# Global attention tasks without TensorE transposes: 32x32 blocks on VectorE, a pass through DRAM, and all later transfers in written order

## The chip, the core and the metric

The program runs on one core of a Trainium2 chip. A core has a matrix engine (TensorE, PE in the profile, with its weight loads as PEld), VectorE (DVE), ScalarE (ACT), GpSimd (POOL) and a queue engine (SyncE, SP) that here issues nearly every DMA. The metric is the device time of one execution in microseconds, the median of several. The kernel before took 911.14 us (three runs, 910.88 to 911.96); the one execution that was profiled took 908.84 us, of which 907.1 us lie between its first and last instruction (its span).

## The reference

Sliding-window attention with a few global tokens, then a feed-forward network with a parametric ReLU, all in float32. There are 8 batches and 8 heads, 512 local and 32 global tokens, head dimension 64. Each global query sees all 544 keys, each local query the 32 global keys and the local keys within 32 positions.

```python
s_g = scale * np.matmul(q_g, k_all.transpose(0, 1, 3, 2))
out_g = np.matmul(sm(s_g), v_all)                 # global queries: 544 keys
...
mask = np.abs(pos[:, None] - pos[None, :]) <= window
s_ll = np.where(mask, s_ll, -1000000000.0)
a_l = sm(np.concatenate([s_lg, s_ll], axis=-1))   # local queries: 32 global + band
out_l = np.matmul(a_l, np.concatenate([v_g, v_l], axis=2))
...
h = x @ w_in                                      # 4352 x 512 by 512 x 2048
g = np.maximum(h, 0.0) + alpha * np.minimum(h, 0.0)
return g @ w_out
```

## The kernel before

**The feed-forward part** sets the beat. Tokens come in nine groups: group b (0 to 7) is the 512 local tokens of batch b, group 8 the 256 global tokens of all batches. A group is worked off in 16 chunks of 128 hidden units; T = 16 * group + chunk numbers the steps. In step T TensorE makes the chunk's hidden values (`f1`: 12 matmuls into a PSUM bank `h_ps`, three for each quarter of the model dimension, because each float32 product is split into a rounded part and a rest: tiles `xh`, `xl`, `wt`), ScalarE and VectorE apply the parametric ReLU (`leak`, `bend`: tile `g`), ScalarE rounds it (`gh`), GpSimd makes the rest (`gl`), and TensorE adds the chunk of two steps ago to the output banks `o` (`f2`: 8 matmuls with `gh`, then 4 with `gl`). When a group is done its four `o` banks are copied to tiles `ost` and stored.

**Local attention** runs between these matmuls, by pairs P of heads, four pairs to a batch, 32 in all. Pairs 0 to 7 go by TensorE transposes; from pair 8 on (`NRAW`) VectorE turns the probabilities in 32x32 blocks (`give`: tile `pb`), SP writes that to DRAM and reads it back with the blocks in their places (`take`: tile `pt`, four transfers for each head), and the values' weighted sum (`local_values`, PSUM tile `o_ps`) follows some steps later. The outputs go the same way (`xb`, then `x_raw`). Inputs of a pair are `qk` (672 KB, one buffer from pair 4 on) and `vw` (two transfers of 512 KB, one buffer from pair 4 on).

**Global attention** is 16 tasks k of two head pairs each. `global_scores` fills part of two PSUM tiles `g_ps` with a large negative number (VectorE memset), multiplies queries and keys (`gn`), and makes row maxima, exponentials (into `sg_sb`, which lies in the buffer of `gn`) and reciprocals of the sums. `global_transposes` turns the probabilities with four 128x128 TensorE transposes into a PSUM tile `gt`, which ScalarE and VectorE copy to `sgt_sb`; the last 32 keys are turned by VectorE directly. `global_values` multiplies with `vg` into `go`, and ScalarE scales it into the two diagonal blocks of `og_sb`, whose other blocks are zero. `global_outputs` turns that on TensorE by a matmul with a matrix `pick` of two unit matrices (`gx`), and ScalarE copies it to `x_glb`, the input of group 8.

**What sets the order.** Up to step 18 a string `ORDER` writes it out: a letter and a number for each piece (S scores, R maxima, E exponentials, V values, F `f1`, A and B the two halves of `f2`, r `leak`, g `bend`, d and e the two heads of `local_exchange`, G `global_scores`). After that TensorE's order is the program's; the piece of a pair or task is put into a step ahead of `f2`'s first half ("pre" before `f1`, "mid") or between its halves ("post"). VectorE, ScalarE and GpSimd are then ordered by a scheduler that simulates the program at build time, with a higher priority for attention. For SP the same holds: after its first loads `dma.on` is False, so that the scheduler places the transfers, except inside `local_exchange`, which switches it on and back. Each queue runs its instructions strictly in order, so that a transfer that waits holds up all behind it. Tiles of 128x512 share one pool of 21 buffers; `h_ps`, `o_ps` and `go` share two PSUM banks, `s_ps`, `g_ps`, `gt` and `gx` two others.

Pair P's values stand in step T = 4 * (P - 4), "post", and behind them the scores of pair P + 1. Task k's scores stand in "mid" of step u, its values in "mid" of step v, the next task's u. Before the change:

```python
plan(u - 2, "mid", load_gn, k)
plan(u, "mid", global_scores, k)
plan(u + 1, "mid", load_vg, k)
plan(v - 2, "mid", global_transposes, k)
at.setdefault((v, "mid"), []).insert(0, (global_values, k))
plan(v + 1, "mid", global_outputs, k)
```

Nearly all instructions are issued through small helpers, so the profile's lines are theirs: L78 is VectorE, ScalarE and SP, L109 TensorE's matmuls, L112 its transposes, L475 GpSimd's `gl`. Tiles tell them apart.

Of the kernel before, what the change touches and what calls it, by code (L numbers as in the profile page):

```python
# [8 lines left out]
F32 = mybir.dt.float32  # L9
# [5 lines left out]
ALU = mybir.AluOpType  # L15
# [18 lines left out]
PAD = (32, 32)  # L34
# [12 lines left out]
    N7 k15 l14 X7 B11 s15 x7 H13 F14 H12 j15 A12 L12 u15 r14 l15 B12 g14 F15 d8 e8 L13 A13 r15 H14  # L47
    g15 H15 B13 L15 L14 F16 r16 g16 H16 L16 A14 V8 S9 B14 N8 R9 F17 p9 r17 q9 g17 d9 A15 B15 e9 H17
# [36 lines left out]
def longformer_ffn(ctx: ExitStack, tc: tile.TileContext, qk, vs, gn, vg, w, alpha, out):  # L85
# [22 lines left out]
    def matmul(*a, **k):  # L108
        return tc.keep_in_program_order(nc.tensor.matmul(*a, **k))  # L109

    def transpose(*a):
        return tc.keep_in_program_order(nc.tensor.transpose(*a))  # L112
# [13 lines left out]
    def bank(tag, name):  # L126
        return psum.tile([128, 512], F32, tag=tag, name=name, bufs=2 if tag in "hs" else 1)
# [20 lines left out]
    vec.tensor_tensor(pick, ident[:, 0:64], ident[:, 64:128], op=ALU.add)  # L148
# [3 lines left out]
    nc.gpsimd.memset(og_sb, 0.0)  # L152
# [148 lines left out]
    def local_exchange(P, heads=(0, 1)):  # L301
        on, dma.on = dma.on, True
        for h in heads:
            ps_of[P, h] = give(pr_of.pop((P, h)), "pb")
        if 1 in heads:
            for h in range(2):
                pt_of[P, h] = stage("pt")
                take(pt_of[P, h], ps_of.pop((P, h)))
        dma.on = on
# [49 lines left out]
    gns, vgs, sgs, gz = {}, {}, {}, {}  # L359
# [13 lines left out]

    def global_scores(k):
        ss = [bank("s", "g_ps") for h in range(2)]
        for h in range(2):
            vec.memset(ss[h][64:128, 256:288], -3.0e38)
# [21 lines left out]
        vec.tensor_copy(z[64:128, 2:4], z[0:64, 2:4])  # L399
        gz[k] = z  # L400

    def global_transposes(k):
        ps, sg_sb = bank("s", "gt"), sgs.pop(k)
        for h in range(2):
            for e in range(2):
                c = 256 * h + 128 * e
                transpose(ps[:, c : c + 128], sg_sb[:, h, 128 * e : 128 * e + 128], ident)
        for h in range(2):
            dst = sgt_sb[:, 0:4, h].rearrange("k (r e) n -> k r e n", r=2)
            copy("ad"[h], dst, ps[:, 256 * h : 256 * h + 256].rearrange("k (e r n) -> k r e n", e=2, r=2))  # L410
# [192 lines left out]
    others = {"R": local_maxima, "E": local_exps, "C": local_copies, "N": local_weights, "x": round_x, "y": rest_x, "D": local_exchange, "p": lambda P: local_exps(P, (0,)), "q": lambda P: local_exps(P, (1,)), "d": lambda P: local_exchange(P, (0,)), "e": lambda P: local_exchange(P, (1,)), "G": global_scores, "h": take_high, "k": take_low, "s": shift, "j": first_join, "u": upper, "l": lower, "r": leak, "g": bend, "H": round_g, "L": rest_g}  # L603
# [81 lines left out]
```

## Time and profile before

| | |
|---|---|
| median of three runs | 911.14 us |
| the profiled execution | 908.84 us |
| its span, first to last instruction | 907.1 us |
| TensorE busy | 889.9 us (98%) |
| VectorE busy | 439.0 us (48%) |
| ScalarE busy | 387.7 us (43%) |
| GpSimd busy | 163.3 us (18%) |
| granted TensorE clock, mean | 0.994 |
| DMA, bytes moved | 140.33 MB |

A row of the groups' view names line, engine, operation, out<-in, partitions x elements, then the count, busy time in us, mean ns of one, and the engine's idle time before them with what ended it. A row of the timeline has start and duration in us, engine, line, operation, tiles, and in brackets the idle time before it and what ended it. Matmuls overlap, so a matmul's cost is the distance from its start to the next one's. One float32 matmul that isn't rounded stands as two instructions. The table by stretches gives, for each, its length, then each engine's busy time with its instructions in brackets, the granted clock, the DMA engines' busy share and GB/s.

### The profile page before, as it was taken

The page shows a single profiled execution, that of the slowest core. Times are in us where ns is not written, and L with a number is a line of the kernel's source. Part 1 is how long each engine was busy: PE and PEld are TensorE (multiplying, and loading weights), DVE is VectorE, ACT ScalarE, POOL GpSimd, SP SyncE. Part 2 cuts the span into 40 slices and gives each one's busy share as a digit, 9 for nine tenths or more (in the row PEclk, how much of TensorE's full clock was granted, in tenths as well). Part 3 has the DMA queues.
Part 4 walks back from the last instruction along what each step waited for, and adds up shares of the span by engine and source line. Part 5 has one row for each costly group of instructions (what it writes and reads, how often), then busy time and mean ns, then how long its engine had stood idle before and what let it go on. Part 6 is the DMA issues. An engine that isn't in the chain of part 4 may idle for free.

```text
span 907.1 us, 21212 instructions
## 1 busy us (share of the span) xinstructions
PE 889.9 (98%) x8704; PEld 718.6 (79%) x8704; DVE 439.0 (48%) x840; ACT 387.7 (43%) x1078; POOL 163.3 (18%) x158
## 2 busy tenths in 40 slices
PE   8889999999999999999999999999999999999998
PEld 4568787787878778877888788877887888888898
DVE  6899996455454444454354434554454323111311
ACT  5786783334443334443343344343343233222322
POOL 3000000211212122112111221122112222222221
PEclk9999999999999999999999999999999999999999
DMA  9994235565446543754546454664535320100000
GB/s 329 342 408 189 81 110 166 183 203 182 159 143 209 183 155 123 246 192 160 180 147 211 149 171 148 213 205 164 185 123 180 112 93 24 46 1 1 12 36 25
DMA packets 139953, 140.33 MB, mean 155 GB/s; under 512 B 9296, under 2 KB 112208, under 8 KB 137808
## 3 DMA queue, kind: packets, MB, share of 16 engines
q1 hardware_dynamic: 139568, 138.72, 45.6%
q8 instruction: 68, 1.11, 0.5%
q14 instruction: 29, 0.24, 0.1%
q10 hardware_dynamic: 288, 0.26, 0.1%
HBM read 111.16 MB, written 27.79 MB: 153 GB/s over the span
## 4 chain that ended last, share of the span: by engine, by line
PE 92%; DMA 3%; SPq 3%; DVE 2%; ACT 0%; issue 0%; DVEq 0%
PE o L109 41%; PE h_ps L109 40%; PE s_ps L109 4%; PE o_ps L109 3%; SPq L78 3%; DMA qk<-in_qk_dram 2%; PE go L109 1%; PE g_ps L109 1%; DMA ws<-in_w_dram 1%; DVE wt L78 1%; PE gt L112 1%; PE pt L112 0%; PE gx L109 0%; ACT wt L78 0%; DVE xl L78 0%
## 5 line engine op out<-in xcount | busy, mean ns | idle before, releaser
L109 PE MATMUL h_ps<-xh,wt 128*128 128x512 f32 (+1 forms) x1152 | 340.0, 378 | 0.0
L475 POOL TENSOR_TENSOR gl<-g,gh 128x512 fp32r<-128x512 f32 (+1 forms) x128 | 156.0, 1219 | 737.0 <-ACT gh L78 632.5
L109 PE MATMUL o<-gh,wt 128*128 128x512 f32 (+1 forms) x1152 | 277.7, 383 | 0.0
L78 DVE SCALAR_TENSOR_TENSOR g<-g,beta_sb,h_ps 128x512 f32<-128x512 f32 (+1 forms) x144 | 102.3, 711 | 317.5 <-ACT g L78 316.2
L109 PEld LDWEIGHTS h_ps<-xh,wt 128*128 128x128 f32 x1152 | 212.0, 188 | 41.9 <-DVE wt L78 0.4
L109 PEld LDWEIGHTS o<-gh,wt 128*128 128x128 f32 x1152 | 204.7, 188 | 44.2 <-issue 6.3
L109 PE MATMUL h_ps<-xl,wt 128*128 128x512 f32 (+1 forms) x576 | 217.7, 378 | 0.0
L78 ACT ACTIVATE g<-h_ps 128x512 f32<-128x512 f32 (+1 forms) x144 | 82.1, 571 | 263.0 <-PE h_ps L109 228.4
L109 PE MATMUL o<-gl,wt 128*128 128x512 f32 (+1 forms) x576 | 151.3, 384 | 0.2 <-DVE gl L78 0.2
L109 PEld LDWEIGHTS h_ps<-xl,wt 128*128 128x128 f32 x576 | 108.4, 188 | 20.0
L78 ACT CAST gh<-g 128x512 fp32r<-128x512 f32 (+1 forms) x144 | 85.7, 597 | 87.3 <-DVE g L78 81.9
L109 PEld LDWEIGHTS o<-gl,wt 128*128 128x128 f32 x576 | 102.9, 188 | 23.4 <-issue 4.4
L78 ACT ACTIVATE p<-p,mn 128x128 f32<-128x128 f32 x192 | 74.5, 390 | 103.3 <-DVE mn L78 70.8
L78 DVE STREAM_TRANSPOSE pb<-p 128x512 f32<-128x512 f32 x48 | 34.1, 711 | 44.0 <-ACT p L78 43.2
L109 PEld LDWEIGHTS o_ps<-vw,pt 128*32 128x32 f32 x2048 | 31.3, 112 | 13.9 <-issue 7.2
L78 DVE TENSOR_TENSOR xq<-o_ps,rz 128x512 f32<-128x512 f32 x32 | 22.1, 691 | 40.0 <-PE o_ps L109 39.2
L109 PE MATMUL s_ps<-qk 64*32 64x128 f32 x2048 | 37.8, 278 | 0.6 <-DMA qk<-in_qk_dram 0.6
L109 PE MATMUL o_ps<-vw,pt 128*32 128x64 f32 x2048 | 36.7, 224 | 1.6 <-DMA pt<-pb 1.6
L78 ACT ACTIVATION_READ_ACCUMULATOR p<-p,mn 128x1 f32 x192 | 36.0, 188 | 0.0
L109 PEld LDWEIGHTS s_ps<-qk 64*32 64x32 f32 x2048 | 29.1, 107 | 6.6 <-issue 2.5
L78 DVE TENSOR_REDUCE mn<-p 128x4 f32<-128x512 f32 x48 | 30.5, 660 | 0.1
L78 DVE SCALAR_TENSOR_TENSOR p<-s_ps,mask 128x512 f32<-128x512 f32 x48 | 30.2, 664 | 0.0
(83 smaller groups left out, 541.2 us busy)
## 6 DMA issues: line engine op xcount, KB each, us to landing
vw<-in_vs_dram SPq DMA_DIRECT2D x64, 512.0 KB, 5.3
qk<-in_qk_dram SPq DMA_DIRECT2D x32, 672.0 KB, 6.6
ws<-in_w_dram SPq DMA_DIRECT2D x16, 1024.0 KB, 9.6
pb<-pb SPq DMA_DIRECT2D x48, 256.0 KB, 2.3
pt<-pb SPq DMA_DIRECT2D x192, 64.0 KB, 2.0
vg<-in_vg_dram SPq DMA_DIRECT2D x32, 320.0 KB, 3.5
gn<-in_gn_dram SPq DMA_DIRECT2D x32, 288.0 KB, 4.4
out_dram<-ost SPq DMA_DIRECT2D x32, 256.0 KB, 3.4
```

What stands on the lines that cost most here:

```text
L78: ins = call(*a, **k)
L109: return tc.keep_in_program_order(nc.tensor.matmul(*a, **k))
L112: return tc.keep_in_program_order(nc.tensor.transpose(*a))
L475: (vec if T < NF else nc.gpsimd).tensor_tensor(gl[:, 0:n], gs.pop(T)[:, 0:n], gh_of[T][:, 0:n].bitcast(F32), op=ALU.subtract)
```

## The change

Six things are changed.

1. `global_transposes` has no TensorE part. VectorE turns the two heads' 256 columns in 32x32 blocks into a tile `sgb` of the common pool (two instructions), SP writes it to DRAM (256 KB) and reads it into `sgt_sb` with four transfers of 64 KB. The layout of `sgt_sb` changes with it. It stands in step u + 1 in place of v - 2.
2. `global_outputs` is eight 32x32 VectorE transposes from `og_sb` to `x_glb` in place of a matmul and a copy; `og_sb` is 64 columns, scaled by one ScalarE instruction in place of two; `pick` and the zeroing of `og_sb` are gone.
3. `global_fill`, the memset of `g_ps`, is a piece of its own: in step u - 1, "post", and for the first task (`f0`) ahead of `H17`.
4. `local_exchange` leaves `dma.on` True: from its first use on (`d8`) SP's transfers stand in the order in which the program writes them.
5. The loads of pair 9's `vw` and pair 10's `qk` stand behind `F18`; `gn` of task k + 1 is loaded behind task k's transposes and `vg`.
6. `d8 e8` stand ahead of `g14 F15` in place of behind them.

```diff
-    N7 k15 l14 X7 B11 s15 x7 H13 F14 H12 j15 A12 L12 u15 r14 l15 B12 g14 F15 d8 e8 L13 A13 r15 H14
-    g15 H15 B13 L15 L14 F16 r16 g16 H16 L16 A14 V8 S9 B14 N8 R9 F17 p9 r17 q9 g17 d9 A15 B15 e9 H17
+    N7 k15 l14 X7 B11 s15 x7 H13 F14 H12 j15 A12 L12 u15 r14 l15 B12 d8 e8 g14 F15 L13 A13 r15 H14
+    g15 H15 B13 L15 L14 F16 r16 g16 H16 L16 A14 V8 S9 B14 N8 R9 F17 p9 r17 q9 g17 d9 A15 B15 e9 f0 H17
...
     def local_exchange(P, heads=(0, 1)):
-        on, dma.on = dma.on, True
+        dma.on = True
...
-        dma.on = on
...
+    def global_fill(k):
+        gps[k] = [bank("s", "g_ps") for h in range(2)]
+        for h in range(2):
+            vec.memset(gps[k][h][64:128, 256:288], -3.0e38)
...
     def global_scores(k):
-        ss = [bank("s", "g_ps") for h in range(2)]
-        for h in range(2):
-            vec.memset(ss[h][64:128, 256:288], -3.0e38)
+        ss = gps.pop(k)
...
     def global_transposes(k):
-        ps, sg_sb = bank("s", "gt"), sgs.pop(k)
+        sg_sb, blk = sgs.pop(k), stage("sgb")
+        for h in range(2):
+            dst = blk.rearrange("k (b h c n) -> k h c b n", b=4, h=2, c=2)[:, h]
+            vec.transpose(dst, sg_sb[:, h, 0:256].rearrange("q (c b n) -> q c b n", c=2, b=4))
         for h in range(2):
             for e in range(2):
-                c = 256 * h + 128 * e
-                transpose(ps[:, c : c + 128], sg_sb[:, h, 128 * e : 128 * e + 128], ident)
-        for h in range(2):
-            dst = sgt_sb[:, 0:4, h].rearrange("k (r e) n -> k r e n", r=2)
-            copy("ad"[h], dst, ps[:, 256 * h : 256 * h + 256].rearrange("k (e r n) -> k r e n", e=2, r=2))
-            for e in range(2):
-                vec.transpose(sgt_sb[0:32, 4, h, 32 * e : 32 * e + 32], sg_sb[32 * e : 32 * e + 32, h, 256:288])
+                vec.transpose(sgt_rest[0:32, h, 32 * e : 32 * e + 32], sg_sb[32 * e : 32 * e + 32, h, 256:288])
+        spread = dram.tile([128, 4, 128], F32, tag="sgb", name="sgb", bufs=2)
+        dma.dma_start(spread, blk.rearrange("k (b n) -> k b n", b=4))
+        for b in range(4):
+            dma.dma_start(sgt_main[32 * b : 32 * b + 32].rearrange("k (w n) -> k w n", w=4), spread[:, b].rearrange("(w k) n -> k w n", w=4))
...
         z = gz.pop(k)
-        for h in range(2):
-            hs = slice(64 * h, 64 * h + 64)
-            act.activation(og_sb[hs, hs], ps[hs, 0:64], AF.Copy, scale=z[hs, 2 + h : 3 + h])
+        act.activation(og_sb, ps[:, 0:64], AF.Copy, scale=z[:, 2:3])
 
     def global_outputs(k):
-        ps = bank("s", "gx")
         b, p = divmod(2 * k, NPAIR)
-        matmul(ps[:, 64:128], og_sb, pick, start=True, stop=True)
-        act.copy(x_glb[:, p : p + 2, SG * b : SG * b + SG], ps[:, 64:128].rearrange("d (e q) -> d e q", e=2))
+        for h in range(2):
+            for e in range(2):
+                for i in range(2):
+                    r0, q0 = 64 * h + 32 * i, 64 * h + 32 * e
+                    vec.transpose(x_glb[r0 : r0 + 32, p + e, SG * b : SG * b + SG], og_sb[q0 : q0 + 32, 32 * i : 32 * i + 32])
...
         if k:
-            plan(u - 2, "mid", load_gn, k)
+            plan(u - 1, "post", global_fill, k)
             plan(u, "mid", global_scores, k)
+        plan(u + 1, "mid", global_transposes, k)
         plan(u + 1, "mid", load_vg, k)
-        plan(v - 2, "mid", global_transposes, k)
+        if k + 1 < NPR // 2:
+            plan(u + 1, "mid", load_gn, k + 1)
         at.setdefault((v, "mid"), []).insert(0, (global_values, k))
-        plan(v + 1, "mid", global_outputs, k)
+        at.setdefault((v + 1, "mid"), []).insert(0, (global_outputs, k))
...
     def first_scores(P, warm):
         local_scores(P, warm)
-        if P > NRAW:
-            load_v(P)
-        if P >= NPAIR:
+        if NPAIR <= P <= NRAW:
             load_qk(P + 1)
...
         if T == NF:
             load_gn(0)
+        if T == NF + 2:
+            load_v(NRAW + 1)
+            load_qk(NRAW + 2)
```

How the built programs' orders differ is shown at three places. First SP in the steady part, from the loads of one pair to those of the next task, as it was and as it is now. Names are those of the tiles: `xb` and `x_raw` carry a pair's outputs, `pb` and `pt` the next pair's probabilities, `vw` and `qk` its values and the inputs of the pair after it.

```order
L78 DMA vw<-in_vs_dram 128x8x128 x2
L78 DMA xb<-xb 128x512
L78 DMA qk<-in_qk_dram 128x1344
L78 DMA x_raw<-xb 32x4x128 x4
L78 DMA pb<-pb 128x512 x2
L78 DMA pt<-pb 32x4x128 x8
L78 DMA vg<-in_vg_dram 128x640 x2
L78 DMA gn<-in_gn_dram 128x576 x2
```

```order
L78 DMA xb<-xb 128x512
L78 DMA x_raw<-xb 32x4x128 x4
L78 DMA pb<-pb 128x512 x2
L78 DMA pt<-pb 32x4x128 x8
L78 DMA vw<-in_vs_dram 128x8x128 x2
L78 DMA qk<-in_qk_dram 128x1344
L78 DMA sgb<-sgb 128x512
L78 DMA sgt_sb<-sgb 32x4x128 x4
L78 DMA vg<-in_vg_dram 128x640 x2
L78 DMA gn<-in_gn_dram 128x576 x2
```

The loads `vw` and `qk` have moved from ahead of the outputs and the probabilities to behind them, and five transfers of the task have come in ahead of `vg` and `gn`. Where a group ends, its four stores `out_dram<-ost` now stand between `qk` and `sgb`.

Second VectorE where pair 8's probabilities are turned (`d8 e8`), as a piece of the difference; `wt` is the last chunk's weights, `xl` the rest of group 1's inputs.

```order
 L78 TENSOR_TENSOR gl<-g,gh 128x512
 L78 TENSOR_TENSOR wt<-wt 128x2x512
+L78 STREAM_TRANSPOSE pb<-p 128x4x4x32 x2
 L78 SCALAR_TENSOR_TENSOR g<-g,beta_sb,h_ps 128x512
 L78 TENSOR_TENSOR xl<-x_raw,xh 128x512 x4
-L78 STREAM_TRANSPOSE pb<-p 128x4x4x32 x2
 L78 TENSOR_TENSOR gl<-g,gh 128x512
 L78 SCALAR_TENSOR_TENSOR g<-g,beta_sb,h_ps 128x512
```

The two transposes have moved ahead of one `bend` and four `xl`.

Third TensorE at the first task's transposes, before and now; `o_2171` and the like are output banks of the feed-forward part.

```order
L109 MATMUL h_ps<-xl,wt 128x512
L112 MATMUL gt<-ident,gn 128x128 x4
L109 MATMUL o_2171<-gh,wt 128x512 x2
L109 MATMUL o_2172<-gh,wt 128x512 x2
L109 MATMUL o_2173<-gh,wt 128x512 x2
L109 MATMUL o_2174<-gh,wt 128x512 x2
L109 MATMUL o_ps<-vw,pt 32x64 x32
```

```order
L111 MATMUL h_ps<-xl,wt 128x512
L111 MATMUL o_2168<-gh,wt 128x512 x2
L111 MATMUL o_2169<-gh,wt 128x512 x2
L111 MATMUL o_2170<-gh,wt 128x512 x2
L111 MATMUL o_2171<-gh,wt 128x512 x2
L111 MATMUL o_ps<-vw,pt 32x64 x32
L111 MATMUL s_ps<-qk 32x128 x32
```

The four transposes are gone, and so is the matmul `gx<-pick,og_sb` of each task at another place; nothing else on TensorE has changed its place.

More of the change, by code (lines that the diff above doesn't have):

```diff
@@ L33 @@
 HPU = 4
-PAD = (32, 32)
+PAD = (32, 32, 0)
 LAG = 2
@@ L99, in longformer_ffn @@
     beta_sb = const.tile([128, NF], F32, name="beta_sb")
-    pick = const.tile([128, 64], F32, name="pick")
-    og_sb = const.tile([128, 128], F32, name="og_sb")
-    sgt_sb = const.tile([128, 5, 2, 64], F32, name="sgt_sb")
+    og_sb = const.tile([128, 64 + PAD[2]], F32, name="og_sb")[:, 0:64]
+    sgt_sb = const.tile([128, 640], F32, name="sgt_sb")
+    sgt_main = sgt_sb[:, 0:512]
+    sgt_cut = sgt_main.rearrange("k (r e h c n) -> k r e h c n", r=2, e=2, h=2, c=2)
+    sgt_rest = sgt_sb[:, 512:640].rearrange("k (h n) -> k h n", h=2)
     x_raw = const.tile([128, NPAIR, SL], F32, name="x_raw")
@@ L147, in longformer_ffn @@
     vec.tensor_scalar(beta_sb, alpha_sb, -1.0, 1.0, op0=ALU.mult, op1=ALU.add)
-    vec.tensor_tensor(pick, ident[:, 0:64], ident[:, 64:128], op=ALU.add)
     band(mask_bf.rearrange("q (i n) -> q i n", i=4), -8.0 * NEG)
@@ L151, in longformer_ffn @@
     nc.gpsimd.memset(sgt_sb, 0.0)
-    nc.gpsimd.memset(og_sb, 0.0)
     def keep_warm(ps, n, add=False):
@@ L357, in rest_x @@
         vec.tensor_tensor(xl, ps_of.pop(P), xh.bitcast(F32), op=ALU.subtract)
-    gns, vgs, sgs, gz = {}, {}, {}, {}
+    gns, vgs, sgs, gz, gps = {}, {}, {}, {}, {}
     big = []
@@ L419, in global_values @@
                     q0 = 64 * h + 32 * e
-                    matmul(ps[q0 : q0 + 32, 0:64], sgt_sb[:, y, h, 32 * e : 32 * e + 32], vgs[2 * k + e][:, y, 64 * h : 64 * h + 64], start=(y == 0), stop=(y == 4))
+                    wt = sgt_cut[:, y // 2, e, h, y % 2] if y < 4 else sgt_rest[:, h, 32 * e : 32 * e + 32]
+                    matmul(ps[q0 : q0 + 32, 0:64], wt, vgs[2 * k + e][:, y, 64 * h : 64 * h + 64], start=(y == 0), stop=(y == 4))
         for e in range(2):
@@ L423, in global_values, with global_outputs @@
         z = gz.pop(k)
+        act.activation(og_sb, ps[:, 0:64], AF.Copy, scale=z[:, 2:3])
+    def global_outputs(k):
+        b, p = divmod(2 * k, NPAIR)
         for h in range(2):
-            hs = slice(64 * h, 64 * h + 64)
-            act.activation(og_sb[hs, hs], ps[hs, 0:64], AF.Copy, scale=z[hs, 2 + h : 3 + h])
-    def global_outputs(k):
-        ps = bank("s", "gx")
-        b, p = divmod(2 * k, NPAIR)
-        matmul(ps[:, 64:128], og_sb, pick, start=True, stop=True)
-        act.copy(x_glb[:, p : p + 2, SG * b : SG * b + SG], ps[:, 64:128].rearrange("d (e q) -> d e q", e=2))
+            for e in range(2):
+                for i in range(2):
+                    r0, q0 = 64 * h + 32 * i, 64 * h + 32 * e
+                    vec.transpose(x_glb[r0 : r0 + 32, p + e, SG * b : SG * b + SG], og_sb[q0 : q0 + 32, 32 * i : 32 * i + 32])
     def split_x(G, c):
@@ L602, in longformer_ffn @@
     on_tensor = {"S": first_scores, "T": local_transposes, "V": first_values, "X": local_outputs, "F": first_f1, "A": lambda T, n: f2(T, 0, n), "B": lambda T, n: f2(T, 1, n)}
-    others = {"R": local_maxima, "E": local_exps, "C": local_copies, "N": local_weights, "x": round_x, "y": rest_x, "D": local_exchange, "p": lambda P: local_exps(P, (0,)), "q": lambda P: local_exps(P, (1,)), "d": lambda P: local_exchange(P, (0,)), "e": lambda P: local_exchange(P, (1,)), "G": global_scores, "h": take_high, "k": take_low, "s": shift, "j": first_join, "u": upper, "l": lower, "r": leak, "g": bend, "H": round_g, "L": rest_g}
+    others = {"R": local_maxima, "E": local_exps, "C": local_copies, "N": local_weights, "x": round_x, "y": rest_x, "D": local_exchange, "p": lambda P: local_exps(P, (0,)), "q": lambda P: local_exps(P, (1,)), "d": lambda P: local_exchange(P, (0,)), "e": lambda P: local_exchange(P, (1,)), "f": global_fill, "G": global_scores, "h": take_high, "k": take_low, "s": shift, "j": first_join, "u": upper, "l": lower, "r": leak, "g": bend, "H": round_g, "L": rest_g}
     for word in ORDER.split():
```

2 lines of the change are left out of this document (1 added, 1 removed).

## The prediction

> **What bounds the kernel now.** I read first the busy shares and the chain that ended last, then the table by stretches, then TensorE's timeline around the pieces that the change touches.
>
> ```profile
> PE 889.9 (98%) x8704; PEld 718.6 (79%) x8704; DVE 439.0 (48%) x840; ACT 387.7 (43%) x1078; POOL 163.3 (18%) x158
> PE 92%; DMA 3%; SPq 3%; DVE 2%; ACT 0%; issue 0%; DVEq 0%
> ```
>
> TensorE is busy for 98% of the span and makes 92% of the chain. Where its idle time lies, the stretches tell.
>
> ```profile
> 0.00:150.00 150.00, 139.77 (x1623) 103.94 (x1624) 130.29 (x184) 108.09 (x258) 7.27 (x30) 0.97 0.67 238
> 150.00:168.00 18.00, 14.74 (x195) 11.35 (x194) 9.81 (x19) 7.01 (x24) 1.95 (x2) 1.00 0.59 195
> 168.00:745.00 577.00, 577.00 (x5952) 464.65 (x5952) 265.80 (x586) 229.66 (x712) 116.46 (x91) 1.00 0.52 170
> ```
>
> From 168 to 745 us, where 15 of the 16 global tasks' scores and all their transposes lie, TensorE has no gap (577.00 of 577.00) at a granted clock of 1.00, while VectorE works 265.80 us, under half. A matmul that leaves this stretch shortens it by its own start-to-start distance, so long as nothing new makes TensorE wait. Just ahead of it, from 150 to 168, TensorE idles 3.26 us.
>
> **The change part by part.** *The task's TensorE work.* Two groups leave, 64 transposes `gt` and 32 instructions `gx`:
>
> ```profile
> L112 PE MATMUL gt<-ident,gn 128*128 128x128 f32 x64 | 9.6, 271 | 0.0
> L109 PE MATMUL gx<-pick,og_sb 128*128 128x64 f32 x32 | 5.3, 247 | 0.0
> 206.78:232.69 25.91, 25.91 (x284) 20.70 (x283) 12.12 (x29) 9.57 (x32) 5.14 (x4) 1.00 0.54 177
> 257.27:283.66 26.39, 26.39 (x288) 21.10 (x287) 12.62 (x32) 11.09 (x35) 5.18 (x5) 1.00 0.65 214
> ```
>
> Their busy times, 14.9 us together, overlap their neighbours and are too much. The two stretches run from one pair's values to the next pair's; both hold a task's values, the next scores and one `gx`, and differ by the four `gt` (x284 against x288). So four `gt` cost 26.39 - 25.91 = 0.48 us. For `gx` the timeline is enough, a step with it beside one without:
>
> ```profile
> 172.61 1.98 PE L109 MATMUL o<-gh,wt 128*128 128x512 f32 x8
> 174.42 1.07 PE L109 MATMUL o<-gl,wt 128*128 128x512 f32 x4
> ...
> 198.72 0.33 PE L109 MATMUL gx<-pick,og_sb 128*128 128x64 f32 x2
> 198.87 2.07 PE L109 MATMUL o<-gh,wt 128*128 128x512 f32 x8
> 200.77 1.07 PE L109 MATMUL o<-gl,wt 128*128 128x512 f32 x4
> ```
>
> From `gx` to the `gl` half 2.05 us, without it 1.81: 0.24 us. Sixteen tasks give 16 x (0.48 + 0.24) = **11.5 us**.
>
> *What VectorE and ScalarE get instead.*
>
> ```profile
> L78 DVE STREAM_TRANSPOSE pb<-p 128x512 f32<-128x512 f32 x48 | 34.1, 711 | 44.0 <-ACT p L78 43.2 <-DMA vw<-in_vs_dram 0.8
> L78 DVE STREAM_TRANSPOSE sgt_sb<-gn 32x32 f32<-32x32 f32 x64 | 12.8, 200 | 12.4 <-ACT gn L78 11.5
> L78 DVE COPY sgt_sb<-gt 128x256 f32<-128x256 f32 x16 | 6.7, 417 | 0.0
> 277.96 0.60 ACT L78 ACTIVATE g<-h_ps 128x512 f32<-128x512 f32 x1 [4.42 <-DMA out_dram<-ost]
> ```
>
> The eight turns into `x_glb` have the form of the 200 ns row: 1.60 us. The two turns into `sgb` have 256 columns each, which no row shows: between 0.20 and 0.71 us; I take half of the 512-column row, 0.36 each, since its elements are twice theirs. With the copy gone VectorE gains 1.60 + 0.72 - 0.42 = 1.9 us a task, 30 us in all, and stays near 51% of the steady stretch. ScalarE loses two copies and one of two scalings. Behind the new VectorE work stands a `bend`, which frees a bank for TensorE and feeds `gh` and `gl`. The last row shows how late it may be: there the activation ahead of it came 4.42 us late for a buffer, inside the stretch 257.27 to 283.66, in which TensorE is busy throughout. A delay of at most 2.3 us (1.60 + 0.72) is covered. Were it not, it would cost up to 16 x 2.3 = 37 us.
>
> [...]
>
> *SP's queue.* Five issues a task, and the read waits for the write:
>
> ```profile
> pb<-pb SPq DMA_DIRECT2D x48, 256.0 KB, 2.3
> vw<-in_vs_dram SPq DMA_DIRECT2D x64, 512.0 KB, 5.3
> qk<-in_qk_dram SPq DMA_DIRECT2D x32, 672.0 KB, 6.6
> ...
> 259.90 1.48 SPq L78 DMA_DIRECT2D xb<-xb  x1
> 265.05 1.76 SPq L78 DMA_DIRECT2D x_raw<-xb  x4
> 266.91 0.85 SPq L78 DMA_DIRECT2D pb<-pb  x2
> 269.00 4.83 SPq L78 DMA_DIRECT2D pt<-pb  x8
> ```
>
> `sgb` is as large as one `pb` (0.4 us to issue, 2.3 to land), its four reads are like the `x_raw` row (1.8 us): SP is held 4.5 us, in step u + 1, three steps ahead of the task's values and ahead of `vg`, `gn` and `xb`. The values come three steps later; four steps are 26.39 us (the stretch above), three 19.8: this is hidden.
>
> Moved past more is `vw` and `qk`: they were issued at once after the pair's values and scores, and now stand behind all of the above. The values that wait for them start here:
>
> ```profile
> 257.27 1.10 PE L109 MATMUL o_ps<-vw,pt 128*32 128x64 f32 x64
> 283.66 1.10 PE L109 MATMUL o_ps<-vw,pt 128*32 128x64 f32 x64
> 284.69 1.16 PE L109 MATMUL s_ps<-qk 64*32 64x128 f32 x64
> ```
>
> As an upper bound let the queue run no earlier than in the rows: `pt` is out at 273.83. Three issues of some 0.5 us put `qk` out at 275.3; it lands at 281.9, `vw` at about 280. Wanted are they at 282.9 and 284.0 (0.72 us earlier than before): 2 us to spare. As a lower bound, where no `vg` and `gn` are under way, `xb` no longer has 1 MB of `vw` ahead of it and lands as `pb` does, after 2.3 us in place of 5.1: then 5 us are to spare. I take no wait, and keep 2 us as the margin that can be lost.
>
> *The two waits from 150 to 168.*
>
> ```profile
> 140.70 0.74 DVE L78 SCALAR_TENSOR_TENSOR g<-g,beta_sb,h_ps 128x512 f32<-128x512 f32 x1
> 143.77 1.30 DVE L78 STREAM_TRANSPOSE pb<-p 128x512 f32<-128x512 f32 x2
> 151.35 0.32 PE L109 MATMUL o_ps<-vw,pt 128*32 128x64 f32 x8
> 153.27 0.99 PE L109 MATMUL o_ps<-vw,pt 128*32 128x64 f32 x56 [1.60 <-DMA pt<-pb]
> 154.19 1.16 PE L109 MATMUL s_ps<-qk 64*32 64x128 f32 x64
> ...
> 162.85 0.71 DVE L78 STREAM_TRANSPOSE pb<-p 128x512 f32<-128x512 f32 x1
> 164.25 0.39 PE L109 MATMUL h_ps<-xl,wt 128*128 128x512 f32 x1
> 165.31 0.75 DVE L78 SCALAR_TENSOR_TENSOR g<-g,beta_sb,h_ps 128x512 f32<-128x512 f32 x1 [1.75 <-ACT g L78]
> 166.06 0.12 DVE L78 MEMSET g_ps<- 64x32 f32 x2
> 166.29 0.81 PE L109 MATMUL g_ps<-gn 64*32 64x288 f32 x16 [1.66 <-DVE g_ps L78]
> ```
>
> Pair 8's values take 154.19 - 151.35 = 2.84 us, a covered pair's 284.69 - 283.66 = 1.03: 1.81 us go to the last `pt`. Its transposes now start at 140.7 in place of 143.8, and no `vg` or `gn` stands between; `pt` then lands 3 us earlier, over a second before it is wanted. What is pushed back is one `bend`, by 1.3 us, and four `xl`; the `gl` behind them starts when it did, since the sum ahead of it is the same. The first task's scores wait for a memset that stands behind a `bend`; from the last `h_ps` matmul to them go 2.04 us. With the memset right behind the transpose of 162.85 it is done before that matmul. The change of shape costs 0.32 us at the other tasks:
>
> ```profile
> 191.51 0.39 PE L109 MATMUL h_ps<-xl,wt 128*128 128x512 f32 x1
> 191.83 0.77 PE L109 MATMUL go<-vg,sgt_sb 128*32 128x64 f32 x40
> ```
>
> so 1.72 us go. Both together **3.5 us**; at the least nothing, if other waits step in.
>
> *The rest.* The missing `pick` and one memset (0.3 us of VectorE, 0.2 of GpSimd) lie in the first 6 us, where TensorE then waits for loads; 0, at best 0.2. The loads of pairs 9 and 10 now stand behind pair 9's `pt`, like those of every later pair, and have the same margin: 0.
>
> **The sum**: 11.5 + 3.5 = 15.0 us; span 907.1 - 15.0 = 892.1. The profiled execution took 1.7 us more than its span (908.84), so 893.8; the median of the runs lies 2.3 us above that execution (911.14), so **896 us**, with 894 to 898 for small errors of the terms.
>
> **The rivals.** *The two early waits stay* in another form (a buffer, the chain of transfers): only the 11.5 us come, 899.6 us. For it: many queues change order there at once; against: both named releasers are moved by more than the wait.
>
> *The end of a group eats part.* The four stores, 1 MB, now stand behind `vw` and `qk`, with `sgb` behind them; at 277.96 an activation already waits for such a store. If the margin of 2 us is used up at five such places and 1 to 2 us a place are lost: 901 to 906.
>
> *Slower: loads after the values.* One buffer each for `vw` and `qk`, and a queue in written order: if `qk` takes more than 284.0 - 275.3 = 8.7 us to land, TensorE stands still at each of 22 pairs. At 9.4 us the 15 us are gone; at 10.2 it is 22 x 1.5 = 33 us lost, 929 us. For it the DMA share of 0.65 in the stretch of the rows; against: its median landing of 6.6 us was measured with `vw` and `xb` beside it.
>
> *Slower by VectorE*: were it the bound of the stretch, 16 x (1.9 - 0.72) = 19 us more, 930; against: it idles for over half of it. [...]
>
> *No change*: TensorE's gain is handed to another engine's pace, 911. Against: none is above 48%.
>
> **How the numbers follow.** Forecast 0.57, early waits stay 0.14, group ends 0.16, late loads 0.06, VectorE 0.02, no change 0.05. A difference under 0.2% (1.8 us) can't be told from none. Faster is 0.57 + 0.14 + 0.16 = 0.87, the same 0.05, slower 0.08. The range reaches from 893.5 (the forecast with `gt` and `gx` at a little more, and 0.2 us at the start) into the group-end case, to 904: 0.57 + 0.14 and two thirds of 0.16, about 0.82.
>
> **What would show it.** In the profile after: no `gt` or `gx`; the steady stretch again without a gap, and 25.67 us from one pair's values to the next where it was 26.39 (less 0.72) or 25.91 (less 0.24); `o_ps` of pair 8 in 1.03 us; `g_ps` of the first task without a wait. Wrong would be TensorE waiting for `vw`, `qk` or `pt` in each pair, for a VectorE `g`, or a period that shrinks by less than 0.7 us.

## The result and the profile after

The changed kernel is **slower**, by 0.6%: 915.14 us in the median of 19 runs (911.26 to 918.53), the kernel before 908.81 us in 19 runs beside it (906.42 to 913.69), a ratio of 1.0063 with a 95% interval of 1.0049 to 1.0077. The prediction was 896 us. The profiled execution has a span of 913.6 us, where 907.1 stood before and 892.1 was forecast.

The busy shares and the chain that ended last, then the stretches with the same borders as before:

```profile
PE 882.2 (97%) x8600; PEld 712.0 (78%) x8608; DVE 458.5 (50%) x983; ACT 377.9 (41%) x1030; POOL 162.9 (18%) x157
PE 73%; DMA 14%; SPq 6%; DVE 4%; issue 2%; ACT 1%; DVEq 0%; ACTq 0%
```

```profile
150.00:168.00 18.00, 18.00 (x211) 14.08 (x211) 11.62 (x29) 8.74 (x29) 2.84 (x3) 1.00 0.50 173
168.00:745.00 577.00, 560.76 (x5811) 450.08 (x5810) 282.89 (x719) 216.49 (x656) 114.07 (x89) 0.99 0.59 186
```

TensorE is busy 7.7 us less (889.9 to 882.2), and from 150 to 168 its two gaps are closed. But the steady stretch, which had none, now has 577.00 - 560.76 = 16.2 us, and a fifth of the chain is DMA and SP's queue. TensorE's waits there, with their sum in us, how many, and the longest in us ("issue" means that the profile names no releaser; the other half of the same values waits for `vw` right behind it):

```profile
PE s_ps L111 <- DMA qk<-in_qk_dram: 11.0, 12, 1.5
PE o_ps L111 <- DMA vw<-in_vs_dram: 3.0, 5, 0.9
PE o_ps L111 <- issue: 2.3, 1, 2.3
```

So it is the loads that changed their place. Why they are late stands in SP's timeline; four rows of pair 9's period, four of pair 10's, and the two `qk` of pairs 11 and 12:

```profile
195.66 2.13 SPq L78 DMA_DIRECT2D qk<-in_qk_dram  x1
197.89 0.38 SPq L78 DMA_DIRECT2D sgb<-sgb  x1
204.30 2.28 SPq L78 DMA_DIRECT2D sgt_sb<-sgb  x4
208.58 0.38 SPq L78 DMA_DIRECT2D xb<-xb  x1
...
223.26 0.74 SPq L78 DMA_DIRECT2D qk<-in_qk_dram  x1
224.10 0.38 SPq L78 DMA_DIRECT2D sgb<-sgb  x1
230.77 3.11 SPq L78 DMA_DIRECT2D sgt_sb<-sgb  x4
235.87 0.38 SPq L78 DMA_DIRECT2D xb<-xb  x1
...
251.65 2.17 SPq L78 DMA_DIRECT2D qk<-in_qk_dram  x1
...
272.36 1.58 SPq L78 DMA_DIRECT2D qk<-in_qk_dram  x1
```

`sgb` is issued right behind 1.7 MB of `vw` and `qk`, and its first read can go only 6.4 and 6.7 us later. Until then SP does nothing, and the next pair's `xb`, which was issued 2.6 us after the pair's values, goes out 7.5 us after them (235.87 against the values at 228.35, below). With it everything behind slips, down to the next `vw` and `qk`. Three of four periods hold a task. From one `qk` to the next go 27.6 and 28.4 us with a task between them, 20.7 without one. TensorE needs 25.64 and 24.10 (rows of early loads, below). These two periods therefore add 2 to 3 us of lateness each, and the one without a task gives some back; over the steady stretch the periods with a task, those with a group's end left out, take 26.1 to 28.4 us.

What the lateness does on TensorE, at pairs 11 and 12, from the timeline and, for one stretch, the table by stretches:

```profile
228.35 1.10 PE L111 MATMUL o_ps<-vw,pt 128*32 128x64 f32 x64
230.21 1.15 PE L111 MATMUL s_ps<-qk 64*32 64x128 f32 x64 [0.76 <-DMA qk<-in_qk_dram]
...
255.60 0.55 PE L111 MATMUL o_ps<-vw,pt 128*32 128x64 f32 x16 [2.26 <-issue]
256.93 0.88 PE L111 MATMUL o_ps<-vw,pt 128*32 128x64 f32 x48 [0.78 <-DMA vw<-in_vs_dram]
259.01 1.96 PE L111 MATMUL s_ps<-qk 64*32 64x128 f32 x64 [1.20 <-DMA qk<-in_qk_dram]
```

```profile
258.40:265.20 6.80, 6.19 (x74) 4.97 (x75) 3.88 (x9) 2.18 (x11) 0.00 (x0) 0.50 0.18 59
```

After 4.2 us of standing still, in three pieces, the scores take 1.96 us where they took 1.15. The last row, of the stretches, says why: for 6.8 us the granted clock is 0.50. A second such record lies at 442.7 to 446.1; before the change there was none between 53 and 906 us (a clock of 1.00 in the mean).

### The profile page after: what moved, and what is told of

The parts are those of the page before. It is cut to its first block, busy times and chain, and to the rows that moved or that the text cites. A ratio compares the mean times of both kernels' runs of the same rounds, so it can differ in the third digit from the quotient of the medians.

```text
span 913.6 us, 21261 instructions
## 1 busy us (share of the span) xinstructions
PE 882.2 (97%) x8600; PEld 712.0 (78%) x8608; DVE 458.5 (50%) x983; ACT 377.9 (41%) x1030; POOL 162.9 (18%) x157
## 2 busy tenths in 40 slices
DMA packets 151474, 148.73 MB, mean 163 GB/s; under 512 B 10576, under 2 KB 121680, under 8 KB 149328
## 4 chain that ended last, share of the span: by engine, by line
PE 73%; DMA 14%; SPq 6%; DVE 4%; issue 2%; ACT 1%; DVEq 0%; ACTq 0%
PE o L111 33%; PE h_ps L111 32%; DMA qk<-in_qk_dram 8%; SPq L78 6%; PE s_ps L111 4%; DMA xb<-xb 3%; PE o_ps L111 2%; DVE wt L78 2%; DMA pb<-pb 2%; PE go L111 1%; PE g_ps L111 1%; DMA ws<-in_w_dram 1%; DMA sgb<-sgb 1%; PE pt L114 0%; DVE xl L78 0%
## 5 line engine op out<-in xcount | busy, mean ns | idle before, releaser
L111 PE MATMUL o<-gh,wt 128*128 128x512 f32 (+1 forms) x1152 | 274.3, 380 | 0.0
L111 PEld LDWEIGHTS o<-gh,wt 128*128 128x128 f32 x1152 | 207.0, 188 | 46.1 <-ACT og_sb L78 6.6
L111 PE MATMUL s_ps<-qk 64*32 64x128 f32 x2048 | 39.9, 288 | 12.9 <-DMA qk<-in_qk_dram 11.0
L111 PEld LDWEIGHTS s_ps<-qk 64*32 64x32 f32 x2048 | 30.6, 110 | 20.3 <-issue 15.7
L78 DVE TENSOR_TENSOR xq<-o_ps,rz 128x512 f32<-128x512 f32 x32 | 22.1, 691 | 43.2 <-PE o_ps L111 42.5
L78 ACT ACTIVATE gn<-g_ps,gm 128x288 f32<-128x288 f32 x32 | 15.7, 496 | 40.1 <-DVE gm L78 40.1
```

Of the source, the lines that this page charges most:

```text
L78: ins = call(*a, **k)
```

## The experiments

Theory Q: SP's queue, in written order and with the task's round trip through DRAM (the hop: `sgb` written, `sgt_sb` read back) behind the loads, is a loop longer than TensorE's period. Rivals: B, the DMA engines' bytes (148.73 MB in place of 140.33, share 0.59); V, VectorE's added work comes late; O, written order and late loads are the harm by themselves, without the hop. Every ratio is to the kernel before, run beside it.

**Early loads.** SP's order of before for `vw` and `qk`, all else as changed:

```diff
-            take(x_raw[:, P % NPAIR], give(xq, "xb"))
+            return give(xq, "xb")
...
-    def scores(P):
+    def scores(P, xb=None):
         local_scores(P)
+        if NRAW + 1 < P < NPR - 1:
+            load_qk(P + 1)
+        if xb is not None:
+            take(x_raw[:, (P - 1) % NPAIR], xb)
...
-    def values(P):
+    def pair(P):
         local_values(P)
...
+            load_v(P + 1)
+        xb = local_weights(P)
+        if P + 1 < NPR:
+            scores(P + 1, xb)
...
-            plan(u + 1, "post", load_v, P + 1)
...
-            plan(u + 1, "post", load_qk, P + 2)
```

> The changed kernel with one thing moved back: pair P+1's `vw` stands right behind pair P's values and pair P+2's `qk` right behind pair P+1's scores, as SP had them before the change; all else, the sgb hop and its 8 MB included, stays. Theory Q (SP's queue: behind 1.7 MB of loads the sgb write lands after 6.4 us instead of 2.3, SP waits for it, and the loads of the next period go out later than in this one): sgb now has no load just ahead of it, lands in 2 to 3 us, TensorE's waits for qk and vw (14 us) go, the clock is 1.00 throughout, span about 892, time 1.5 to 1.7% under the kernel before. Theory B (the DMA engines are full: 148.7 MB and a share of 0.59): the same bytes, so still 0.4 to 0.8% slower than before. Theory V (VectorE's added 1.9 us a task come late): nothing changed for it, still 0.4 to 0.8% slower.

892.38 us against 910.01: 0.9804 (0.9780 to 0.9828), **2.0% faster**; span 890.4. The steady stretch with two periods of it, and SP's rows for one `sgb`:

```profile
168.00:745.00 577.00, 577.00 (x5969) 464.78 (x5968) 288.88 (x728) 222.86 (x668) 118.60 (x93) 1.00 0.58 188
201.34:226.98 25.64, 25.64 (x282) 20.48 (x281) 13.34 (x39) 9.55 (x31) 5.15 (x4) 1.00 0.63 199
226.98:251.08 24.10, 24.10 (x226) 19.77 (x225) 10.98 (x17) 10.31 (x30) 5.14 (x4) 1.00 0.59 190
```

```profile
221.92 0.34 SPq L78 DMA_DIRECT2D sgb<-sgb  x1
223.96 1.73 SPq L78 DMA_DIRECT2D sgt_sb<-sgb  x4
```

No gap, a clock of 1.00, periods of 25.64 and 24.10, with the same bytes and the same VectorE work: B and V fall. The read follows the write after 2.0 us, which is also the median landing of `sgb` over the kernel, in the next row; in the changed kernel it is 5.1.

```profile
sgb<-sgb SPq DMA_DIRECT2D x16, 256.0 KB, 2.0
```

**Late reads.** The loads stay late; only the four reads into `sgt_sb` move, behind the next pair's `xb` write:

```diff
-            take(x_raw[:, P % NPAIR], give(xq, "xb"))
+            xb = give(xq, "xb")
+            if spreads:
+                take(sgt_main, spreads.pop())
+            take(x_raw[:, P % NPAIR], xb)
...
-        for b in range(4):
-            dma.dma_start(sgt_main[32 * b : 32 * b + 32].rearrange("k (w n) -> k w n", w=4), spread[:, b].rearrange("(w k) n -> k w n", w=4))
+        spreads.append(spread)
```

> The changed kernel with the four reads into sgt_sb moved behind the next pair's `xb` write; the loads stay late, behind pt, and the sgb write stays right behind them. Theory Q: SP no longer stops for the sgb landing (6.2 of the 27.6 us between one qk and the next), so the loop is about 21.4 us, under the 25.64 that TensorE takes for a period; waits for qk and vw go, span 892 to 895, 1.3 to 1.7% faster than before. A weaker form of Q, that the place of the loads alone is too late: the waits are halved, span 900 to 905. Theories B and V: still 0.4 to 0.8% slower.

892.96 us: 0.9810 (0.9787 to 0.9834), span 891.8. The steady stretch:

```profile
168.00:745.00 577.00, 576.52 (x5966) 464.07 (x5965) 289.05 (x726) 222.16 (x667) 119.04 (x93) 1.00 0.58 188
```

With the four transfers whose wait stopped SP in another place, the loss is gone; the loads may stand late, as long as SP comes to them in time. The landing itself is better too: `sgb` takes 2.1 us in the median, where the changed kernel has 5.1, as SP now runs ahead and waits for VectorE's `sgb` at all 16 tasks (at 9 in the changed kernel), so that the write goes out some 5 us behind `qk` (223.34 after 218.29). This suggests that part of the long landing in the changed kernel comes of SP being late.

**Written order only.** The tasks' TensorE transposes, copies and `pick` matmul as before; written order, late loads and the early edits kept. Beside the three functions:

```diff
-        plan(u + 1, "mid", global_transposes, k)
...
+        plan(v - 2, "mid", global_transposes, k)
         at.setdefault((v, "mid"), []).insert(0, (global_values, k))
-        at.setdefault((v + 1, "mid"), []).insert(0, (global_outputs, k))
+        plan(v + 1, "mid", global_outputs, k)
```

> The changed kernel with the global tasks' TensorE transposes, the pick matmul, their copies and their places taken back from before; written order of the transfers, late loads and the early edits stay, the sgb hop is gone. Theory Q: without the hop the queue's loop is 27.6 - 6.4 - 1.9 = 19.3 us against a period of 26.39, no TensorE wait for qk; only the early edits count, -3.5 us, span 903 to 904, 0.4% faster than before. Theory O (written order and late loads are the harm by themselves): TensorE waits for qk or vw as in the changed kernel, 14 us, span 915 or more, 1% slower than before. Theory V: no wait, as Q.

905.03 us: 0.9947 (0.9926 to 0.9967), span 902.6; the steady stretch is busy 576.58 of 577.00. O falls. The early edits are worth 907.1 - 902.6 = 4.5 us here, and what is left to early loads, 902.6 - 890.4 = 12.2 us, is the tasks' TensorE work (the difference of two kernels, each with runs 4 to 5 us apart; the periods below agree with it).

**Order found at build time.** One switch of the change undone, `dma.on` put back behind `local_exchange`:

```diff
-        dma.on = True
+        on, dma.on = dma.on, True
...
+        dma.on = on
```

> The changed kernel with the one switch undone that keeps SP in written order: dma.on is put back behind local_exchange, so the order of the transfers is again found at build time; it puts vw, xb, qk ahead of x_raw, pb and pt as before the change, and sgb behind vg and gn of the task. Theory Q: no waits for qk or vw in the steady stretch, 1.3 to 1.7% faster than before; if the early edits need the written order, 1.2%. Theories B and V: still 0.4 to 0.8% slower.

894.59 us: 0.9825 (0.9801 to 0.9849), span 892.9, no gap in the steady stretch. So either of two edits undone, the switch or the loads' new place, turns the loss into a gain of 1.7 to 2%. Here `sgb` stands behind `vg` and `gn` and lands after 4.9 us in the median, nearly as late as in the changed kernel (in the steady stretch SP waits 65.3 us for it in all, there 68.2), and TensorE waits for nothing: a late landing alone is not the loss.

**The hop twice, loads late.** A larger dose, for the size of the loop:

```diff
-        spread = dram.tile([128, 4, 128], F32, tag="sgb", name="sgb", bufs=2)
-        dma.dma_start(spread, blk.rearrange("k (b n) -> k b n", b=4))
+        for hop in range(2):
+            spread = dram.tile([128, 4, 128], F32, tag="sgb", name="sgb", bufs=2)
+            dma.dma_start(spread, blk.rearrange("k (b n) -> k b n", b=4))
...
```

> The changed kernel (late loads) with the sgb hop made twice for each task: written again and read again into the same place, the second time with nothing to add. Theory Q: in the kernel with early loads such a hop holds SP 3.9 us, so the queue's loop in a period with a task goes from 27.9 to about 31.9 us and stays 20.7 without one; over four periods (3 x 31.9 + 20.7) / 4 = 29.1 us against TensorE's (3 x 25.64 + 24.10) / 4 = 25.26, so 22 x 3.84 = 84 us over the 890.4 of early loads: span about 974, 7% slower than before. Theory B (bytes): the first 8.4 MB cost 23 us (913.6 - 890.4), a second 8.4 MB as much again: span 937, 3% slower.

978.23 us: 1.0777 (1.0737 to 1.0817), span 976.4 where Q said 974 and B 937. From one `qk` to the next:

```profile
199.26 0.71 SPq L78 DMA_DIRECT2D qk<-in_qk_dram  x1
231.30 0.91 SPq L78 DMA_DIRECT2D qk<-in_qk_dram  x1
262.28 1.60 SPq L78 DMA_DIRECT2D qk<-in_qk_dram  x1
282.59 1.27 SPq L78 DMA_DIRECT2D qk<-in_qk_dram  x1
```

32.0, 31.0 and 20.3 us: SP's loop sets the time. Over the 16 periods from this first `qk` to the one at 669.90 its mean is 29.4 us, where 29.1 was expected; 22 x (29.4 - 25.26) = 91 us over early loads, against 86 measured.

**The hop twice, loads early.** The same loop in the kernel with early loads.

> The kernel with early loads, again with the sgb hop made twice. Theory Q: SP waits there 49 us for o_ps and 32 us for sgb in the steady stretch, about 3.5 us a period to spare, and the loads have 14 us and more until they are needed; 3.9 us more a task move nothing that TensorE waits for: span 890 to 892, 1.9% faster than before, as with one hop. Theory B: 157 MB, 23 us more than with one hop, span 913.

931.53 us: 1.0244 (1.0224 to 1.0265), span 929.9. Both theories' numbers were wrong, Q's by 39 us. SP's rows of two tasks, and TensorE's waits:

```profile
205.50 0.38 SPq L78 DMA_DIRECT2D sgb<-sgb  x1
...
232.75 0.38 SPq L78 DMA_DIRECT2D sgb<-sgb  x1
```

```profile
PE h_ps L111 <- DVE xl L78: 8.9, 4, 2.8
PE g_ps L111 <- DMA gn<-in_gn_dram: 5.4, 8, 1.2
```

From task to task the loop is 27.2 us here and up to 28.8 in other groups, so 23.3 to 24.9 with one hop: 0.7 to 2.3 us to spare in a task's period, not 3.5. I had averaged SP's idle time over all periods, but time spared in a period without a task is not carried into the next, since SP can't load ahead of a single buffer. And `vw` and `qk`, which I watched, are in time; late now is what stands behind the hop, `gn` and, through `x_raw`, the rests `xl`. Not all of the 39.5 us over early loads is placed: TensorE idles 18.9 us in the steady stretch, and four records of half the clock there hold 13.7 us.

**Standstills on purpose.** Early loads, in which `vw` of four pairs is issued late, behind ever more of SP's transfers:

```diff
+LATE = (10, 14, 18, 22)
...
+        when = {2: "sgb", 5: "sgt", 8: "gn", 11: "hop"}.get(k)
+        for hop in range(1 + (when == "hop")):
...
+            if when == "sgb":
+                load_v(11)
...
+        if when == "sgt":
+            load_v(15)
...
-        if P + 1 < NPR:
+        if P + 1 < NPR and P not in LATE:
             load_v(P + 1)
...
+    for P in LATE[2:]:
+        plan(4 * (P - NPAIR) + 3, "mid", load_v, P + 1)
```

> The kernel with early loads, in which at four pairs, far apart, the next pair's `vw` is issued late on purpose: behind the sgb write (pair 11), behind its four reads (pair 15), behind vg and gn (19), behind a second hop, vg and gn (23). Each time TensorE should stand still once, for about 1, 4, 5 and 9 us, by the queue's times in the kernel with early loads and 5 us of landing. Theory K (the granted clock falls to 0.5 after a standstill of some length): records of 0.5 behind the longer standstills, none behind the first, and the matmuls there last 1.7 times as long; the whole costs more than the standstills add up to, by 2 to 3 us for each such fall. Theory N (the falls in the changed kernel had another cause): no records under 1, the cost is the sum of the standstills, 19 us.

924.75 us in its one run, span 923.0. The kernel has one line more, so TensorE's matmuls are L112. The ends of the four standstills in TensorE's timeline, its waits for `o_ps` in the steady stretch, and the stretches in which the granted clock was 0.50:

```profile
228.44 0.88 PE L112 MATMUL o_ps<-vw,pt 128*32 128x64 f32 x48 [0.37 <-DMA vw<-in_vs_dram]
...
333.02 0.49 PE L112 MATMUL o_ps<-vw,pt 128*32 128x64 f32 x16 [3.71 <-DMA vw<-in_vs_dram]
334.29 1.51 PE L112 MATMUL o_ps<-vw,pt 128*32 128x64 f32 x48 [0.78 <-DMA vw<-in_vs_dram]
...
445.33 0.67 PE L112 MATMUL o_ps<-vw,pt 128*32 128x64 f32 x16 [7.59 <-issue]
...
559.52 0.65 PE L112 MATMUL o_ps<-vw,pt 128*32 128x64 f32 x16 [10.82 <-DMA vw<-in_vs_dram]
```

```profile
PE o_ps L112 <- DMA vw<-in_vs_dram: 17.1, 6, 10.8
PE o_ps L112 <- issue: 7.6, 1, 7.6
```

```profile
333.30:340.10 6.80, 6.02 (x129) 4.78 (x120) 3.65 (x6) 0.27 (x1) 0.00 (x0) 0.50 0.87 287
442.50:449.30 6.80, 3.30 (x112) 2.92 (x119) 1.02 (x2) 0.00 (x0) 0.00 (x0) 0.50 0.39 118
551.70:565.40 13.70, 5.14 (x131) 4.19 (x132) 2.33 (x4) 0.00 (x0) 0.00 (x0) 0.50 0.68 203
```

Theory K holds: no fall behind 0.37 us, one behind each longer standstill. The seven waits sum to 17.1 + 7.6 = 24.7 us, but the span is 923.0 - 890.4 = 32.6 us longer, so a fall cost 7.9 / 3 = 2.6 us on top. The records say the same another way: TensorE is busy in them for 6.02 + 3.30 + 5.14 = 14.5 us, at half speed, which is 7.2 us lost. With one run the figure is an estimate; the spans of early loads' four runs lie 4.5 us apart.

**An eighth of the bytes, loads late.** The same transfers and waits, 32 KB written and 4 x 8 KB read; seven eighths of the turned probabilities are left out, and the values' matmuls read zeros there.

```diff
-        dma.dma_start(spread, blk.rearrange("k (b n) -> k b n", b=4))
+        dma.dma_start(spread[0:16], blk[0:16].rearrange("k (b n) -> k b n", b=4))
...
+            dma.dma_start(sgt_main[32 * b : 32 * b + 16, 0:128], spread[0:16, b])
```

> The changed kernel (late loads) with the sgb hop cut to an eighth of its bytes: one write of 32 KB and four reads of 8 KB, as many transfers and the same waits as before the cut. It leaves out seven eighths of the turned probabilities; the values' matmuls run as before, on zeros there. Theory Q: the wait for the landing behind vw and qk stays, so the sgb write still lands after 5 to 6.4 us, the loop stays over 25.64 us, TensorE still waits for qk: span 908 to 914, no faster than before. Theory B (bytes; DMA 141.4 in place of 148.7 MB): seven eighths of the loss of 23 us go, span 893 to 895, 1.6% faster than before.

900.12 us: 0.9909 (0.9881 to 0.9936), span 899.6, between the two theories. The read still waits for the write behind the loads, but for a shorter time, and the loop shrinks to about TensorE's period:

```profile
194.72 0.67 SPq L78 DMA_DIRECT2D qk<-in_qk_dram  x1
196.75 0.34 SPq L78 DMA_DIRECT2D sgb<-sgb  x1
201.18 1.79 SPq L78 DMA_DIRECT2D sgt_sb<-sgb  x4
...
219.97 0.90 SPq L78 DMA_DIRECT2D qk<-in_qk_dram  x1
```

4.4 us in place of 6.4, and 25.25 us from `qk` to `qk`. What B had right is that bytes count, but through the landings that SP waits for: of the 23.2 us between the changed kernel and early loads, 9.2 remain (this kernel's runs spread more than the others': 895.39 to 907.47 us).

**Twice the bytes, one wait, loads early.**

```diff
         dma.dma_start(spread, blk.rearrange("k (b n) -> k b n", b=4))
+        dma.dma_start(spare, blk.rearrange("k (b n) -> k b n", b=4))
+        for again in range(2):
+            take(sgt_main, spread)
```

> The kernel with early loads, with the hop's bytes doubled and no second wait: sgb is written twice, to two places, and the first is read twice. 157 MB, as in the kernel with early loads and two hops, which took 929.9 us; SP is held 2.3 us more a task, for the issues, in place of 3.9. From that kernel's rows, where the sgb write of one task stands 27.2 to 28.6 us behind that of the task before, the queue's loop with early loads and one hop is 23.3 to 24.7 us; with 2.3 us more it is 25.6 to 27.0, up to 1.4 us over TensorE's 25.64, and gn lands 3.6 us before it is wanted. Theory Q: span 890 to 895, 1.5 to 1.9% faster than before. Theory B: the bytes of the kernel with two hops, so its span, 925 to 930.

897.70 us: 0.9878 (0.9853 to 0.9904), span 898.2, which is the slowest of four runs (893.5 to 898.2): 3 to 8 us over early loads, inside or up to 3 us past what Q allowed, and some 32 us under the kernel with two hops and the same 157 MB. The waits, not the bytes, make up most of that kernel's loss.

**`vg` and `gn` between the hops.** The kernel with two hops and early loads, the second hop moved behind `vg` and `gn`.

```diff
             plan(u + 1, "mid", load_gn, k + 1)
+        plan(u + 1, "mid", second_hop, k)
```

> The kernel with early loads and two hops (929.9 us, where 891 was expected), with vg and gn moved ahead of the second hop: the same transfers and bytes, another order. There TensorE's longer steps, against the kernel with early loads, were go and g_ps (13.9 us in all: vg and gn late) and h_ps (15.9 us). Theory G (vg and gn behind the hop are what costs): the 13.9 us go, span 916. Theory Q (the length of SP's loop costs, whatever stands in it): the second write now queues behind 1.2 MB of vg and gn, which land after 4 to 4.6 us; the hop holds SP 6.3 us in place of 3.9, the loop is 30 to 31 us, over four periods (3 x 30.5 + 20.7) / 4 = 28.0 against 25.26, so 22 x 2.8 = 61 us over early loads: span about 950, slower than with vg and gn behind it.

940.05 us: 1.0370 (1.0330 to 1.0409), span 945.4, the longest of five runs, the others 937.6 to 942.7. The waits for `gn` and `vg` are gone from TensorE's list, and the time is longer, under Q's 950 but far from 916. The longest entry in their place:

```profile
PE go L111 <- DMA sgt_sb<-sgb: 14.5, 7, 2.8
```

Of this wait a part is the experiment's own: the second hop writes `sgt_sb` again, so the task's values wait for it, which Q's number left out. So this run speaks against G, and its size is no clean measure of the loop.

**Early loads and late reads together**, as the version with the most room on SP. In the early loads' `scores`:

```diff
             load_qk(P + 1)
+        if spreads:
+            take(sgt_main, spreads.pop())
         if xb is not None:
             take(x_raw[:, (P - 1) % NPAIR], xb)
```

> The kernel with early loads and the late reads of sgt_sb together, as the version with the most room on SP. Theory Q: TensorE was without a gap in the steady stretch with either, so nothing more is to be had: span 890 to 892, the same as with early loads alone within 0.3%. If the remaining gain depended on SP's room, it would be faster than that.

902.78 us: 0.9933 (0.9907 to 0.9959), span 900.0: 10 us slower than either alone, which no theory had foreseen. The reads now stand right behind `vw`, `xb` and `qk`:

```profile
207.75 0.38 SPq L78 DMA_DIRECT2D qk<-in_qk_dram  x1
208.19 1.87 SPq L78 DMA_DIRECT2D sgt_sb<-sgb  x4
```

```profile
214.73 0.77 PE L111 MATMUL go<-vg,sgt_sb 128*32 128x64 f32 x40 [0.93 <-DMA sgt_sb<-sgb]
```

They stand behind 1.9 MB, and the task's values, which wait for them, start 6.5 us after the first is issued (214.73 after 208.19). Nine such waits make 6.4 of the 8.9 us that TensorE idles in the steady stretch. It is the cause of the changed kernel once more, a small transfer issued right behind large loads, in another place. The fastest version remains early loads, faster than both kernels.

## Why the prediction was wrong

**What held.** *The early waits.* Pair 8's values now take 152.54 - 151.51 = 1.03 us, and the first `g_ps` follows its `h_ps` without a gap:

```profile
151.51 1.10 PE L111 MATMUL o_ps<-vw,pt 128*32 128x64 f32 x64
152.54 1.16 PE L111 MATMUL s_ps<-qk 64*32 64x128 f32 x64
...
162.60 0.39 PE L111 MATMUL h_ps<-xl,wt 128*128 128x512 f32 x1
162.92 0.69 PE L111 MATMUL g_ps<-gn 64*32 64x288 f32 x16
```

Forecast 3.5 us, measured 4.5 in the run with written order only; the difference is within what runs of one kernel differ by. *The tasks' TensorE work.* 25.64 us from pair to pair where 25.67 was forecast; 12.2 us in all, forecast 11.5. *VectorE.* The turns into `sgb` take 0.42 us (0.36 taken), those into `x_glb` 0.20, so 2.0 us more a task (1.9 forecast), covered: with early loads TensorE never waits in the steady stretch. The sum of 15.0 us and its span of 892.1 us are near what early loads gave: 890.4. The 2.3 us added to the forecast for the median was chance: it came from three runs of the kernel before; over 19 runs its median, 908.81, is within 0.1 us of the profiled execution's 908.84.

**The step that failed** is SP's queue, at "`sgb` is as large as one `pb` (0.4 us to issue, 2.3 to land) [...] SP is held 4.5 us". The size was right and the place was not: a `pb` had no load just ahead of it, `sgb` has `vw` and `qk`. SP was held from 224.10 to 233.9, 9.8 us. With 2.0 us to land the term was right, in the kernel with early loads. Right behind the two loads the first read could go 6.4 and 6.7 us after the write (204.30 after 197.89, 230.77 after 224.10); by what mechanism loads delay a write issued behind them was not shown.

The second fault follows from it. I asked of the hop whether the task's values wait for it ("this is hidden"), and of the loads whether one period's `pt` lets them out in time, with "as an upper bound let the queue run no earlier than in the rows". It was no bound: the rows had `xb` 2.6 us after the values, and the hop, still standing ahead of it, made that 7.5. `vw` and `qk` went out 22.1 and 23.3 us after pair 11's values, where I had 18.0 for `qk`. A queue in written order is a loop, and its length (27.6 us) has to be held against the period (25.64); one round of it, started in time, looked hidden.

**The rivals.** The late loads had 0.06. Their condition, a `qk` that takes over 8.7 us to land, wasn't met (6.8 to 7.9 in the rows of four pairs); what was late was its issue, and 12 waits for `qk` and 5 for `vw` stand against 22 pairs, as the lateness grows over three periods and partly drains in the fourth. The end of a group eats part: the four stores do stand ahead of `sgb`, but there `sgb` waits for VectorE, goes out 7.7 us behind the first store (281.74 after 274.04) and lands after 2.0; TensorE's next wait for `qk` or `vw` comes 36 us or more after the stores, at the second pair behind them at the earliest. So these places are not where the time goes. VectorE and no change: not seen.

**The ledger.** From pair 9's values to the last pair's the changed kernel takes 753.12 - 176.47 = 576.65 us, early loads 729.92 - 175.70 = 554.22: 22.4 us more. 16.2 are TensorE's idle time; about 4.5 the slow clock: its two records hold 10.2 us, of which 9.1 lie behind the waits, at half speed. 1.7 us I can't place. The gain of 16.7 us (907.1 - 890.4) less these 22.4 and 0.8 from the start (176.47 - 175.70) gives the 6.5 us between the spans.

## What to carry to other kernels

When transfers are put in written order, add up one full round of the queue, with every wait for a landing, and compare it with the period of the engine that bounds; check each hidden step by what is queued behind it, period after period. Where that round is too long, a write that is read back should not stand right behind large loads (here it held its read up by 6.4 to 6.7 us, and without loads just ahead by 2.0): either put the loads behind it, or put other issues between the write and its read, and look at what the read itself then stands behind. If an added hop loses time, try its place before its removal: here four reads moved past five other transfers made 2.5% (0.9810 against 1.0063).

## What the hardware showed that was not expected

The granted clock fell to 0.50 at standstills of TensorE, in records of 3.4, 6.8 and 13.7 us, and in the run with four standstills it stayed there for 4 to 7 us after the work was back (340.1 against 333.02, 449.3 against 445.33, 565.4 against 559.52). The length of the waits alone does not tell which bring it on: in the changed kernel two of 0.72 and 1.47 us at 440 to 443 did, while two of 0.28 and 1.46 us at 650 to 653 and one of 1.38 us ahead of 547.82 did not; there the clock stayed at 1.00 and the scores took 1.15 us. TensorE was busy for 1.43 us of the 3.4 us just ahead of the first fall (255.0 to 258.4) and for 1.69 us ahead of the second (439.3 to 442.7), and for 1.74 us of the 3.4 us from 251.6 to 255.0, behind which the clock stayed at 1.00 until 258.4. How much idle time brings a fall on was not shown. But a wait on the engine that bounds can cost more than itself: by the estimate above some 2.6 us a fall in the run with four standstills.

The time until a transfer had landed depended less on its size, in these kernels, than on what was issued just ahead: the same 256 KB of `sgb` landed after 2.0 us in the median with early loads, and its read could go 6.7 us after it right behind `vw` and `qk` (230.77 after 224.10). For 32 KB in that place it was 4.4 us (201.18 after 196.75, the kernel with an eighth of the bytes). Reads of 64 KB (`sgt_sb`) landed after 1.9 us in the median with early loads; behind `vw`, `xb` and `qk` in the last experiment TensorE could use the four of them 6.5 us after the first was issued (214.73 after 208.19).
